# A decayed-attention kernel with a feed-forward layer: Strassen's seven products for the second token group, with its weight sums moved and taken from float16

## The chip, the cores and the metric

The kernel runs on one core of a Trainium2 chip. The metric is the device time of one execution in microseconds (us). Four runs of the kernel before gave 205.49 to 206.1 us, median 205.8 us. In this text PE is TensorE (matmul), DVE is VectorE, ACT is ScalarE, POOL is GpSimd and SP is SyncE, which issues most DMAs.

## What is computed

```python
# attention: q, k, v are (4, 8, 768, 64); blocks of 64 positions, one decay lam per head
intra = (q_b @ k_b^T) * lam^(i-j) for i >= j      # inside a block
out_b = intra @ v_b + (q_b * lam^(i+1)) @ state   # state: 64 x 64 per head
state = lam^64 * state + (k_b * lam^(63-j))^T @ v_b
# feed-forward on x = out as (3072, 512)
h = x @ w_in                # 512 -> 2048
g = gelu_tanh(h)
y = g @ w_out               # 2048 -> 512, float32 out
```

## The kernel before, in words

**Attention.** There are 24 steps `s`, each 256 positions of four heads. `prep(s)` makes float16 copies: `prep_qk` scales q on DVE (L237) and copies k on ACT (L242), `prep_v` scales v on POOL (L227). `stage_t(s)` transposes q and k on PE for `s < 9` (L258) and copies the result out of PSUM (L261 to L267; by ACT for 1, 5 and 6, by both for 2 and 3, by DVE for 0, 4, 7 and 8); later steps are transposed by a DMA from SP's queue (L246). `R(n, s)` puts on PE the scores of step n (`Sps`, L287), the key-value products of n (L322) and the outputs of step s (L336, L345), then on DVE the mask (`PT`, L296) and the state (`t`, L381, L384), and on POOL the spread state `u` (L391); `x_out` copies outputs to `xT` on ACT (L364). `U(n)` is the state step for the second block of n.

**Feed-forward.** Two steps of the same positions make one super-block of 256 tokens. The 12 super-blocks form seven groups, `[0,1] [2] [3] [4,5] [6,7] [8,9] [10,11]`; a "256-token group" is one of the second and third. `queue_group(g)` appends a group's PE work in pieces to the list `filler`, and `fill(n)` in the hand-written order at the end of the kernel (L613 to L719) takes the next n pieces. All instructions keep program order on their engine. `mm1` (L415) is one 512-column bank of `x @ w_in` (eight matmuls of 256 columns in a 256-token group) and a gelu on ACT into `gT` (L423). The second matmul has two forms:

- `mm2` (L428), for groups 0 and 1: four matmuls of 512 columns a piece, 16 for each 128 tokens, into one PSUM bank `O2ps`; ACT copies it out (L440), SP sends it.
- `product(m, p)` (L470), for groups 2 to 6: Strassen's scheme on 2 x 2 blocks (tokens by halves, the 2048 by halves, columns by halves). Seven products take the place of eight; each is eight matmuls of 256 columns (L488). Five of them need sums of blocks of g, made on DVE by `sum_g` (L456, L464) from `gT`; five need sums of blocks of w_out, `w_sum16`, made once by `sum_wout(j, m, eng)` (L120, L124) for halves j = 0 and 1. Products 4 and 3 fill PSUM bank A, 5 and 2 bank B, 1 bank C, 7 and 6 bank D. After product 2, ACT copies bank B (L495, L496) and DVE combines it with A (L499, L500); after product 1 DVE adds C (L508), after product 6 it adds D (L520), and SP sends the tile.

The order of the pieces of a 256-token group is eight `mm1`, then products 3, 4, 5, 2, 1, 7, 6. `behind(k, i0, i1)` (L572) hangs `sum_g` for rows i0 to i1 onto the k-th piece: the five sums of rows 0 to 3 follow the sixth `mm1`, the five of rows 4 to 7 follow product 3.

**Weights.** `load_wout` brings w_out in four parts of 512 rows as float32 (order 0, 2, 1, 3). `cast_wout` makes float16 parts in `w_out16`: 0 on POOL, 2 on ACT, 1 and 3 half on POOL and half on ACT (L116, L118). `sum_wout` reads the float32 parts. Before the change its five sums for j = 0 stand after `cast_wout(0)` and ahead of `fill(8)` (L672), those for j = 1 behind `U(8)`, `U(9)` and `U(10)` (L716).

**PSUM.** Six banks (`ps_M`) serve everything but the scores. A new tile takes a bank that an earlier tile gave up, and its first matmul waits until the last reader of the earlier tile is done. Which bank that is gets settled when the program is built.

Of the kernel before, what the change touches and what calls it, by code (L numbers as in the profile page):

```python
# [15 lines left out]
def kernel(  # L16
# [11 lines left out]
    pin = tc.keep_in_program_order  # L28
# [32 lines left out]
    def load_step(s):  # L61
# [3 lines left out]
        for nm, src in (("q", q), ("k", k), ("v", v)):  # L65
# [9 lines left out]
    w_out16 = w16p.tile([P, NF, DM], FP16)  # L75


    HF, HE = NF // 2, DM // 2
    w_sum16 = w16p.tile([P, 5, HF, HE], FP16)
    W_SUMS = {3: ((0, 1), ALU.subtract, (1, 1)), 4: ((1, 0), ALU.subtract, (0, 0)),  # L80
              1: ((0, 0), ALU.add, (1, 1)), 7: ((1, 0), ALU.add, (1, 1)),
              6: ((0, 0), ALU.add, (0, 1))}
    w_slot = {m: i for i, m in enumerate(W_SUMS)}
    wstage = {}
# [25 lines left out]
    def cast_wout(j, eng):  # L110
        t = wstage[("o", j)]
        for i in range(2):
            dst = w_out16[:, 4 * j + 2 * i : 4 * j + 2 * i + 2, :]
            src = t[:, 2 * i : 2 * i + 2, :]
            if eng[i] is nc.scalar:
                pin(nc.scalar.activation(out=dst, in_=src, func=AF.Copy))  # L116
            else:
                pin(nc.gpsimd.tensor_copy(out=dst, in_=src))  # L118

    def sum_wout(j, m, eng):  # L120

        (f0, e0), op, (f1, e1) = W_SUMS[m]
        a, b = wstage[("o", j + 2 * f0)], wstage[("o", j + 2 * f1)]
        pin(eng.tensor_tensor(w_sum16[:, w_slot[m], 4 * j : 4 * j + 4, :],  # L124
                              a[:, :, e0 * HE : e0 * HE + HE], b[:, :, e1 * HE : e1 * HE + HE], op))


    lam_in = const.tile([H, 1], FP32)
# [85 lines left out]
    def prep(s):  # L214
        prep_qk(s)
        prep_v(s)
# [8 lines left out]
    def prep_v(s):  # L225
        tv = a16p.tile([P, 2, HH, D], FP16, tag="v16", name=f"v16_{s}")
        pin(nc.gpsimd.tensor_tensor(wide(tv[:]), ld32[s][2][:], decay(dv, s), ALU.mult))  # L227
        a16[s] = a16[s] + (tv,)
        if s >= 6:
            load_ahead(s + 3)  # L230

    def prep_qk(s):
        q32, k32, _ = ld32[s]
        tqk = a16p.tile([P, 2, 2, HH, D], FP16, tag="qk16", name=f"qk16_{s}")
        tq, tk = tqk[:, 0], tqk[:, 1]
        q_eng = nc.gpsimd if s == 3 else nc.vector
        pin(q_eng.tensor_tensor(wide(tq), q32[:], decay(dq, s), ALU.mult))  # L237
        if s == 0:
            inverse(halves[0])
            odd(halves[1])  # L240
            inverse(halves[1])
        pin(nc.scalar.activation(out=wide(tk), in_=k32[:], func=AF.Copy))  # L242
        a16[s] = (tq, tk)
        if s >= FIRST_DMA_T:
            o = qkp.tile([P, 2, 2, 2, P], FP16, tag="qkT", name=f"qkT_{s}")
            pin(nc.sync.dma_start_transpose(out=o[:].rearrange("p a j h t -> p (a j h) t"),  # L246
                                            in_=tqk[:].rearrange("p a j h d -> p (a j h d)")))
            qkT[s] = o

    def stage_t(s):  # L250
        if s >= FIRST_DMA_T:
            return
        tq, tk = a16[s][:2]
        Tps = ps_M.tile([P, 2, 2, 2, P], FP16, tag="M", name="Tps")
        for i, t in enumerate((tq, tk)):
            for hp in range(2):
                for j in range(2):
                    pin(nc.tensor.transpose(Tps[:, i, j, hp, :], t[:, j, 2 * hp : 2 * hp + 2, :],  # L258
                                            ident[:]))
        o = qkp.tile([P, 2, 2, 2, P], FP16, tag="qkT", name=f"qkT_{s}")  # L260
        if s in (2, 3):  # L261
            pin(nc.scalar.activation(out=o[:, 0], in_=Tps[:, 0], func=AF.Copy))
            pin(nc.vector.tensor_copy(out=o[:, 1], in_=Tps[:, 1]))
        elif s in (1, 5, 6):
            pin(nc.scalar.activation(out=o[:], in_=Tps[:], func=AF.Copy))
        else:
            pin(nc.vector.tensor_copy(out=o[:], in_=Tps[:]))  # L267
        qkT[s] = o
# [131 lines left out]
    filler = []  # L400

    def queue_group(g):
        N = len(groups[g]) * SB
        NTAU = N // P
# [10 lines left out]
        def mm1(fs):  # L415
            Hps = ps_M.tile([P, per, N], FP32, tag="M", name="Hps")
            for i, f in enumerate(fs):
                for c in range(NC):
                    pin(nc.tensor.matmul(by_block(Hps[:, i, :]), w_in16[:, c, f * P : (f + 1) * P],  # L419
                                         x(c), start=(c == 0), stop=(c == NC - 1)))  # L420
            f = fs[0]
            dst = gT[:, f, :, :] if per == 2 else gT[:, f % HF, f // HF : f // HF + 1, :]
            pin(nc.scalar.activation(out=dst, in_=Hps[:], func=AF.Gelu_apprx_tanh))  # L423
# [4 lines left out]
        def mm2(tau, part):  # L428

            if not O2.get(tau):  # L430
                O2[tau] = [ps_M.tile([P, DM], FP32, tag="M", name="O2ps"), 0]
            for f in range(4 * part, 4 * part + 4):
                n = O2[tau][1]
                pin(nc.tensor.matmul(O2[tau][0][:], gT[:, f % HF, f // HF, tau * P : (tau + 1) * P],  # L434
                                     w_out16[:, f, :], start=(n == 0), stop=(n == NF - 1)))
                O2[tau][1] += 1
            if O2[tau][1] < NF:
                return
            o32 = otp.tile([P, DM], FP32, tag="o32", name="o32")
            pin(nc.scalar.activation(out=o32[:], in_=O2.pop(tau)[0][:], func=AF.Copy))  # L440
            pin(nc.sync.dma_start(out=out[row0 + tau * P : row0 + tau * P + P, :], in_=o32[:]))
# [11 lines left out]
        def block(T, F, i):  # L453
            return gT[:, i, F, T * HN : (T + 1) * HN]

        def sum_g(i0, i1):  # L456
            for m, ((T0, F0), op, (T1, F1)) in G_SUMS.items():
                if m not in gsum:
                    k = len(gsum)
                    if k % 2 == 0:  # L460
                        pairs.append(wst.tile([P, 2, HF, HN], FP16, tag="w32", name=f"gs_{g}_{m}"))
                    gsum[m] = pairs[-1][:, k % 2]
                i = slice(i0, i1)
                pin(nc.vector.tensor_tensor(gsum[m][:, i, :], block(T0, F0, i), block(T1, F1, i), op))  # L464
# [92 lines left out]
        for i in range(HF):  # L557
            for fs in ([[i, i + HF]] if per == 2 else [[i], [i + HF]]):
                filler.append(lambda fs=fs: mm1(fs))
        if g == 1:  # L560
            for tau in range(NTAU):
                for part in (0, 2, 1, 3):
                    filler.append(lambda tau=tau, part=part: mm2(tau, part))
            return
        ms = ((3, 4, 5, 2), (1, 7, 6))
        order = [(m, p) for p in range(HN // P) for m in ms[0] + ms[1]]
        if g == len(groups) - 1:
# [1 line left out]
        for m, p in order:  # L569
            filler.append(lambda m=m, p=p: product(m, p))  # L570

        def behind(k, i0, i1):  # L572

            piece = filler[at + k]

            def both():
                piece()
                sum_g(i0, i1)

            filler[at + k] = both  # L580

        at = len(filler) - len(range(HN // P)) * 7 - HF * (2 // per)
        n1 = HF * (2 // per)
        if per == 2:
            behind(5, 0, 4)
            behind(n1, 4, 8)
        else:
            behind(9, 0, 4)
            behind(13, 4, 6)
            behind(n1, 6, 8)  # L590

    def fill(n):
        for _ in range(min(n, len(filler))):
            filler.pop(0)()

    def R(n, s):
        if n is not None:
            scores(n)
        products(n, s)
        if n is not None:  # L600
            causal(n)
        if s is not None and s % 2 == 1:
            g, i = group_of[s // 2]
            if i == len(groups[g]) - 1 and g > 0:
                queue_group(g)
        if n is not None:
            update(n, 0)

    def U(n):
        update(n, 1)  # L610
# [58 lines left out]
        cast_win(j)  # L669
    DVE, ACT, POOL = nc.vector, nc.scalar, nc.gpsimd  # L670
    cast_wout(0, (POOL, POOL))
    for m in W_SUMS:  # L672
        sum_wout(0, m, DVE)
    fill(8)
    cast_wout(2, (ACT, ACT))
    cast_wout(1, (POOL, ACT))
    cast_wout(3, (POOL, ACT))
    fill(9)
    prep(4)
    stage_t(4)  # L680
    prep(5)
    fill(2)
    R(4, None)
    stage_t(5)
# [4 lines left out]
    stage_t(6)  # L689
    U(5)  # L690
    prep(7)
    fill(2)
    R(6, 5)
    U(6)
# [1 line left out]
    prep(8)  # L696
    fill(1)
    stage_t(7)
    fill(2)
    R(7, 6)  # L700
    U(7)
# [3 lines left out]
    for n in range(8, NSTEP + 1):  # L705
        m = n if n < NSTEP else None
        if m is not None:
            stage_t(n)
        if n + 2 < NSTEP:
            prep(n + 2)  # L710
        fill(2 if n <= 12 else 4)
        R(m, n - 1)
        fill(1)
        if m is not None:
            U(m)
        for p in {8: (3, 4), 9: (1, 7), 10: (6,)}.get(n, ()):  # L716
            sum_wout(1, p, DVE)
        fill(2 if n == 11 or n > 12 and n % 2 else 3)
    fill(len(filler))  # L719

# [28 lines left out]
```

## Time and profile before

| what | value |
|---|---|
| median of 4 runs | 205.8 us |
| the profiled execution | 205.92 us |
| its span in the profile | 204.1 us |
| what lies around the span | 1.82 us |
| granted PE clock | 1.0 |
| PE busy, instructions | 197.1 us (97%), 2324 |
| DVE busy | 146.1 us (72%) |
| ACT busy | 107.9 us (53%) |
| POOL busy | 68.9 us (34%) |
| `mm2` of all groups (L434) | 96 matmuls of 512 columns |
| `sum_wout` (L124) | 10 instructions, 14.8 us |

Times inside the profile are microseconds from the span's start. A row of the groups gives line, engine, operation, what it writes and reads, the shapes, the count, then busy time, mean nanoseconds of one, and the idle time ahead of them with what ended it. A row of the timeline or of the chain gives start, length, and what ran. A duration in the timeline counts from when an instruction was at the head of its engine, so one that was held up shows longer than the same instruction alone.

### The profile page before, as it was taken

How to read it: one execution, taken by the hardware profiler on the slowest of the kernel's cores; microseconds unless marked ns; L12 is line 12 of the kernel's file. 1: busy time of each engine (PE TensorE's matmuls, PEld its weight loads, DVE VectorE, ACT ScalarE, POOL GpSimd, SP SyncE). 2: the span in 40 equal slices, each digit the busy share in tenths (PEclk: the TensorE clock that was granted, in tenths of full speed). 3: DMA queues.
4: the chain of work that ended last, by engine and by line, in shares of the span. 5: the costliest groups of instructions: out<-in, count | busy, mean ns of one | idle time of the engine just before them, and what ended most of it. 6: DMA issues, size and time to landing. Idle time of an engine off the chain costs nothing.

```text
span 204.1 us, 5592 instructions
## 1 busy us (share of the span) xinstructions
PE 197.1 (97%) x2324; PEld 128.7 (63%) x2324; DVE 146.1 (72%) x274; ACT 107.9 (53%) x204; POOL 68.9 (34%) x80
## 2 busy tenths in 40 slices
PE   6988999999999999999999999999999999999993
PEld 1556544456885688644688654688654788545882
DVE  5799726867699999929997828996739773136552
ACT  2365678466873573477723377631576431666210
POOL 6486132446587850336044304214412101000000
PEclk9999999999999999999999999999999999999999
DMA  6999999999999999996449983658340003300014
GB/s 168 293 330 385 387 386 376 280 281 318 326 245 229 290 247 143 234 283 177 89 123 250 236 241 100 144 114 135 84 99 0 0 3 103 108 0 0 3 51 154
DMA packets 63945, 37.85 MB, mean 185 GB/s; under 512 B 17584, under 2 KB 59056, under 8 KB 63920
## 3 DMA queue, kind: packets, MB, share of 16 engines
q1 hardware_dynamic: 63088, 36.97, 68.8%
q10 hardware_dynamic: 832, 0.52, 0.8%
q8 instruction: 18, 0.29, 0.6%
q14 instruction: 7, 0.06, 0.1%
HBM read 27.26 MB, written 6.29 MB: 164 GB/s over the span
## 4 chain that ended last, share of the span: by engine, by line
PE 92%; DMA 2%; DVE 2%; ACT 1%; issue 1%; SPq 0%
PE Hps L419 37%; PE O2ps L434 10%; PE MB L488 8%; PE MA L488 7%; PE MD L488 7%; PE Sps L287 4%; PE MC L488 4%; PE OK L345 3%; PE Hps L534 3%; PE OK L336 3%; PE Tps L258 2%; DMA k<-in_k_dram 2%; PE idle L152 2%; PE OK L322 1%; ACT qk L242 1%; DVE PT L296 1%
## 5 line engine op out<-in xcount | busy, mean ns | idle before, releaser
L419 PE MATMUL Hps<-xT,w_in 128*128 128x512 f16 (+1 forms) x416 | 79.1, 346 | 0.0
L423 ACT ACTIVATE gT<-Hps 128x512 f16<-128x512 f32 x88 | 52.4, 596 | 22.8 <-PE Hps L419 22.0
L419 PEld LDWEIGHTS <-w_in 128*128 128x128 f16 x416 | 40.3, 98 | 33.4
L391 POOL TENSOR_TENSOR u<-t,lumask 128x256 f16<-128x256 f32 x40 | 31.3, 789 | 81.8 <-DVE t L384 53.8
L464 DVE TENSOR_TENSOR gs<-gT 128x512 f16<-128x512 f16 (+1 forms) x70 | 36.6, 586 | 10.8 <-ACT gT L423 10.6
L296 DVE TENSOR_TENSOR PT<-Sps,mask 128x1024 f16<-128x1024 f32 x24 | 29.2, 1215 | 16.9 <-PE Sps L287 16.8
L488 PEld LDWEIGHTS <-gs 128*128 128x128 f16 x360 | 34.9, 98 | 4.0
L227 POOL TENSOR_TENSOR v<-v,dv 128x512 f16<-128x512 f32 x24 | 29.5, 1230 | 4.9 <-DMA v<-in_v_dram 2.6
L364 ACT ACTIVATE xT<-OK 128x256 f16<-128x256 f32 x47 | 18.1, 454 | 20.7 <-PE OK L345 16.3
L434 PE MATMUL O2ps<-w_out,gT 128*128 128x512 f16 x96 | 21.9, 379 | 0.0
L495 ACT ACTIVATE m<-MB 128x512 f32<-128x512 f32 x9 | 5.4, 597 | 25.4 <-PE MB L488 25.4
L237 DVE TENSOR_TENSOR qk<-q,dq 128x512 f16<-128x512 f32 x23 | 18.3, 798 | 0.0
L242 ACT ACTIVATE qk<-k 128x512 f16<-128x512 f32 x24 | 15.0, 623 | 6.4 <-DMA k<-in_k_dram 6.4
L488 PE MATMUL MA<-w_sum,gT 128*128 128x256 f16 x144 | 17.5, 273 | 0.1
L488 PE MATMUL MD<-w_sum,gs 128*128 128x256 f16 x136 | 17.5, 273 | 0.0
L488 PE MATMUL MB<-w_out,gs 128*128 128x256 f16 x144 | 17.2, 273 | 0.0
L488 PEld LDWEIGHTS <-gT 128*128 128x128 f16 x144 | 14.1, 98 | 2.8 <-ACT gT L423 0.3
L434 PEld LDWEIGHTS <-gT 128*128 128x128 f16 x96 | 9.2, 98 | 9.9
L499 DVE TENSOR_TENSOR o<-MA,m 128x512 f32<-128x512 f32 x9 | 6.2, 689 | 12.7 <-ACT m L495 12.7
L384 DVE SCALAR_TENSOR_TENSOR t<-t,lamu,OK 128x64 f32<-128x64 f32 x64 | 14.6, 272 | 0.9 <-PE OK L322 0.2
L124 DVE TENSOR_TENSOR w_sum<-wo,wo 128x1024 f16<-128x1024 f32 x6 | 8.8, 1507 | 4.6 <-DMA wo<-in_moe_w_out_dram 4.6
L287 PEld LDWEIGHTS <-qkT 64*64 64x64 f16 x384 | 6.3, 108 | 8.6 <-issue 4.2
(60 smaller groups left out, 170.3 us busy)
## 6 DMA issues: line engine op xcount, KB each, us to landing
q<-in_q_dram SPq DMA_DIRECT2D x24, 256.0 KB, 5.0
k<-in_k_dram SPq DMA_DIRECT2D x24, 256.0 KB, 5.0
v<-in_v_dram SPq DMA_DIRECT2D x23, 256.0 KB, 5.2
out_dram<-o SPq DMA_DIRECT2D x22, 256.0 KB, 4.0
wo<-in_moe_w_out_dram SPq DMA_DIRECT2D x4, 1024.0 KB, 9.1
wi<-in_moe_w_in_dram SPq DMA_DIRECT2D x4, 512.0 KB, 7.5
wi<-in_moe_w_in_dram SPq DMA_DIRECT2D x2, 1024.0 KB, 12.6
v<-in_v_dram ACTq DMA_DIRECT2D x1, 256.0 KB, 4.5
```

The lines of the kernel that those rows point to most:

```text
L227: pin(nc.gpsimd.tensor_tensor(wide(tv[:]), ld32[s][2][:], decay(dv, s), ALU.mult))
L237: pin(q_eng.tensor_tensor(wide(tq), q32[:], decay(dq, s), ALU.mult))
L242: pin(nc.scalar.activation(out=wide(tk), in_=k32[:], func=AF.Copy))
L296: pin(nc.vector.tensor_tensor(t[:].rearrange("p a b c d -> p (a b) (c d)"), Ss.pop(n)[:].rearrange("p a b c d -> p (a b) (c d)"), mask[:]. ...
L364: pin(nc.scalar.activation(out=d, in_=o, func=AF.Copy))
L384: pin(nc.vector.scalar_tensor_tensor(t[:, hp, :], state[half][:, hp, :], lamu[:, 2 * half + hp : 2 * half + hp + 1], K[:, hp, :], ALU.mult ...
L391: pin(nc.gpsimd.tensor_tensor(u[:], state[half][:].unsqueeze(2).to_broadcast([P, 2, 2, D]), lumask[:, 2 * half : 2 * half + 2, :].unsqueez ...
L419: pin(nc.tensor.matmul(by_block(Hps[:, i, :]), w_in16[:, c, f * P : (f + 1) * P], x(c), start=(c == 0), stop=(c == NC - 1)))
L423: pin(nc.scalar.activation(out=dst, in_=Hps[:], func=AF.Gelu_apprx_tanh))
L434: pin(nc.tensor.matmul(O2[tau][0][:], gT[:, f % HF, f // HF, tau * P : (tau + 1) * P], w_out16[:, f, :], start=(n == 0), stop=(n == NF - 1)))
L464: pin(nc.vector.tensor_tensor(gsum[m][:, i, :], block(T0, F0, i), block(T1, F1, i), op))
L488: pin(nc.tensor.matmul(dst, lhsT, rhs, start=(i == 0), stop=(i == HF - 1), skip_group_check=True))
```

## The change

1. Group 1 gets the seven products in place of its eight `mm2` pieces (the `if g == 1` branch goes). 32 matmuls of 512 columns become 56 of 256 columns.
2. In both 256-token groups the sums of g are spread: `sum_g` takes a list `ms`. Sums 5 and 2 for rows 0 to 3 follow the sixth `mm1`; sum 5 for rows 4 to 7 follows the eighth; sum 2 for rows 4 to 7 follows product 3; sums 1 and 7 over all rows follow product 4; sum 6 over all rows follows product 5. So sums 1, 7 and 6 stand ahead of the combinations behind product 2 in DVE's queue.
3. `sum_wout` reads `w_out16` (float16) and not the float32 parts. It now waits for the casts. For j = 0 the sums stand after the casts, in the order 6, 3, 4, 1, 7, then that of j = 1 for product 6; the other four of j = 1 follow `prep(5)`, `prep(7)` and (two) `stage_t(7)`.
4. The transposes of step 8 are copied out by ACT and not by DVE.
5. The `fill` behind `U(8)` takes two pieces and not three, since group 1 has 15 pieces and not 16.

```diff
     def sum_wout(j, m, eng):
         (f0, e0), op, (f1, e1) = W_SUMS[m]
-        a, b = wstage[("o", j + 2 * f0)], wstage[("o", j + 2 * f1)]
-        pin(eng.tensor_tensor(w_sum16[:, w_slot[m], 4 * j : 4 * j + 4, :],
-                              a[:, :, e0 * HE : e0 * HE + HE], b[:, :, e1 * HE : e1 * HE + HE], op))
+        def rows(f, e):
+            f = f * HF + 4 * j
+            return w_out16[:, f : f + 4, e * HE : e * HE + HE]
+        pin(eng.tensor_tensor(w_sum16[:, w_slot[m], 4 * j : 4 * j + 4, :], rows(f0, e0), rows(f1, e1), op))
...
-        elif s in (1, 5, 6):
+        elif s in (1, 5, 6, 8):
             pin(nc.scalar.activation(out=o[:], in_=Tps[:], func=AF.Copy))
...
-        def sum_g(i0, i1):
+        def sum_g(i0, i1, ms=None):
             for m, ((T0, F0), op, (T1, F1)) in G_SUMS.items():
+                if ms and m not in ms:
+                    continue
...
-        if g == 1:
-            for tau in range(NTAU):
-                for part in (0, 2, 1, 3):
-                    filler.append(lambda tau=tau, part=part: mm2(tau, part))
-            return
...
         if per == 2:
-            behind(5, 0, 4)
-            behind(n1, 4, 8)
+            behind(5, 0, 4, (5, 2))
+            behind(7, 4, 8, (5,))
+            behind(8, 4, 8, (2,))
+            behind(9, 0, 8, (1, 7))
+            behind(10, 0, 8, (6,))
...
     cast_wout(0, (POOL, POOL))
-    for m in W_SUMS:
-        sum_wout(0, m, DVE)
     fill(8)
     cast_wout(2, (ACT, ACT))
     cast_wout(1, (POOL, ACT))
     cast_wout(3, (POOL, ACT))
+    for m in (6, 3, 4, 1, 7):
+        sum_wout(0, m, DVE)
+    sum_wout(1, 6, DVE)
     fill(9)
     prep(4)
     stage_t(4)
     prep(5)
+    sum_wout(1, 3, DVE)
...
     prep(7)
+    sum_wout(1, 4, DVE)
...
     stage_t(7)
+    sum_wout(1, 1, DVE)
+    sum_wout(1, 7, DVE)
...
-        for p in {8: (3, 4), 9: (1, 7), 10: (6,)}.get(n, ()):
-            sum_wout(1, p, DVE)
-        fill(2 if n == 11 or n > 12 and n % 2 else 3)
+        fill(2 if n in (8, 11) or n > 12 and n % 2 else 3)
```

More of the change, by code (lines that the diff above doesn't have):

```diff
@@ L570, in queue_group, with behind @@
             filler.append(lambda m=m, p=p: product(m, p))
-        def behind(k, i0, i1):
+        def behind(k, i0, i1, ms=None):
             piece = filler[at + k]
@@ L577, in both @@
                 piece()
-                sum_g(i0, i1)
+                sum_g(i0, i1, ms)
             filler[at + k] = both
```

## The prediction, on record before the result

> **What bounds the kernel now.** I read the page's busy shares and slices first, then the chain of work that ended last, then the timelines of DVE and POOL around the second group.
>
> ```profile
> PE 197.1 (97%) x2324; PEld 128.7 (63%) x2324; DVE 146.1 (72%) x274; ACT 107.9 (53%) x204; POOL 68.9 (34%) x80
> ...
> DVE  5799726867699999929997828996739773136552
> ```
>
> PE is busy for 97%. A slice is 5.1 us; DVE is full from about 56 to 87 us, where the second group's second matmul stands. In order of time the chain is PE without a gap from 21.7 us to 200.6 us, but for a wait near 76 us.
>
> ```profile
> 60.57 4.32 PE O2ps L434 x20
> 64.89 0.35 PE Sps L287 x16
> ...
> 65.92 2.59 PE O2ps L434 x12
> 68.51 2.62 PE Hps L419 x24
> ...
> 75.73 0.45 issue
> 76.18 0.62 ACT qk L242
> 76.80 0.49 ACT gT L423
> 77.29 0.05 issue
> 77.34 0.28 PE MA L488
> ...
> 100.56 1.75 PE MA L488 x16
> ```
>
> Columns are start, length, what ran, matmuls. The first and third lines are the 32 matmuls that the change replaces; the last is sixteen of the kind that replaces them. The lines near 76 us are product 3 of group 2 waiting for a gelu queued behind a k copy on ACT: five `mm1` from 72.15 and eight products should end at 77.40 and end at 77.62, so 0.22 us. So PE work taken out shortens the run one for one, if everything that PE waits for is still on time.
>
> **Step 1, the matmuls.** Out: 4.32 + 2.59 = 6.91 us for 32, 0.216 each. In: 56 at 1.75 / 16 = 0.1094, 6.13 us. Gain 0.78 us. The sixteen-matmul rows are 1.75 in every later group, so I give this no range. The Trainium skill, "TensorE: Matmul & The Clock Gate", section "Back-to-back issue gap", speaks against the change: it gives a sustained 131 ns for 512 columns and 81 ns for 128; a straight line between them gives 98 ns for 256, an estimate, and by it 56 x 98 - 32 x 131 ns would make the run 1.3 us longer. This trace has 216 and 109 ns, so the measurement decides.
>
> **Step 2, evacuation.** ACT loses two `O2ps` copies of 0.60 us and gains 0.60 + 0.38 (rows of L495, L496). Output DMAs stay two of 256 KB, issued some 2 us later on SP, ahead of step 12's DMA transpose, which waits for its q until then anyway and is needed at 83 us. Nothing.
>
> **Step 3, DVE's work and POOL.** The sums of w_out change from 1.21 us (float32 alone, 73.29 us) to the row of L464 with the same shapes.
>
> ```profile
> 73.29 1.21 DVE L124 TENSOR_TENSOR w_sum<-wo 128x1024 f16<-128x1024 f32 x1
> 74.43 0.83 DVE L464 TENSOR_TENSOR gs<-gT 128x512 f16<-128x512 f16 x1
> 75.18 1.26 DVE L464 TENSOR_TENSOR gs<-gT 128x512 f16<-128x512 f16 x1
> 76.36 0.41 DVE L464 TENSOR_TENSOR gs<-gT 128x512 f16<-128x512 f16 x1
> ```
> ```profile
> 73.51 1.47 POOL L391 TENSOR_TENSOR u<-t,lumask 128x256 f16<-128x256 f32 x1 [2.21 <-DVE t L384]
> 74.94 1.22 POOL L227 TENSOR_TENSOR v<-v,dv 128x512 f16<-128x512 f32 x1
> ```
>
> Start, length, operation, shapes. Alone, a sum of 512 takes 0.41 us (next one 0.34 on), one of 1024 takes 0.68 (next one 0.60 on), `u` 0.61, `v` 1.04. Here the `u` asked at 73.51 and ended at 74.98, 0.5 after the DVE sum ended at 74.50; the DVE sum asked at 74.43 and ended 0.28 after that `u`; the next ended 0.28 after the `v` (76.16). So a DVE operation with two SBUF inputs and a POOL operation take turns, whole instructions at a time. `PT`, `t` and the bank combinations, which read PSUM, keep 1.21, 0.27 and 0.68 beside POOL. With these turns I laid DVE's new order out by hand, on before's clock.
>
> *28 to 42 us.* The first sum needs `cast_wout(0)` (POOL, done 31.07). The next wait for `cast_wout(2)`, whose second half ends on ACT near 35.6 (33.62 plus two of 1.0). From 35.7: three sums at 0.60, a turn for POOL's cast (asked at 37.34; to 38.5), two sums, end 39.7. Before, the float32 sums ended at 39.7 too:
>
> ```profile
> 39.62 0.68 DVE L237 TENSOR_TENSOR qk<-q,dq 128x512 f16<-128x512 f32 x1
> ```
>
> So step 4's q is ready at 40.3 as before, and its transposes on PE (40.86 in the chain) lose nothing. But `v` of step 4 asks POOL at 39.87: were DVE 0.2 us later, `v` would go first, q end 0.9 later, and PE stand still some 0.65 us.
>
> *42 to 55 us.* The sums behind `prep(5)`, `prep(7)`, `stage_t(7)` fall into idle stretches of DVE (0.80, 0.99, 1.42 us). The first starts at 42.56 while `v` of step 5 asks at 42.59. If the `v` wins, `PT` of step 4 is 0.6 late, then `u`, and PE loses some 0.25. The last two wait for `v` of step 8 and push `PT` of step 7 from 54.33 to 54.5.
>
> *55 to 61 us.* ACT copies step 8's transposes in 1.02 us (row of L265) from 57.1 to 58.2; PE takes them at 58.72. Two gelus are 0.6 and 0.3 late and free of it by 59.7; the gelu of the eighth `mm1` starts at 60.61 as before and ends 61.21, and product 3 reaches its eighth matmul at 61.33: no wait. DVE now takes turns with two `u` and two `v`: q of 9 ends 57.2, q of 10 58.2, first sum 59.3, second 60.5, and `PT` of step 8 starts 60.4, not 59.18.
>
> *61 to 71 us, the tight part.* Against PE's due time without any wait: sum 5 (rows 4 to 7) ready 62.4, due 62.76; sum 2 63.1, due 63.6; sum 1 64.1, due 65.1; sum 7, behind the `v` of step 11, 65.5, due 65.97; sum 6, behind q of 11, 66.7 plus about 0.1 to be seen by PE, due 66.85. The combinations of bank A end 67.9, C 70.05, D 71.05. Six banks are alive here (A, B, step 9's two, C, D). Group 2's first `mm1` (due 67.7) and second (68.6) can have B (free at 65.2 by ACT) and A; the third (69.46) takes step 9's first, free when `t` ends at 69.44. I put 0.1 us of waiting there. So DVE, with 3.3 us of sums of g and 2.5 of combinations in place of 7.5 of float32 sums, is just in time; the margins are 0 to 0.5 us.
>
> *After 71 us* DVE has no w_out sums left (1.21 us less) and fewer sums at once; group 2's order of products and copies is otherwise the same, and the 0.22 us wait near 76 stays, since the k copy is still ahead of the gelu. The end of the kernel is untouched.
>
> **Sum.** Profiled execution 205.92 = 204.1 + 1.82. Minus 0.78, plus 0.1: 205.24. The median of the runs lies 0.12 lower, which would give 205.1; I say **205.2 us**.
>
> **The rivals.**
>
> *DVE late in the tight part.* For: the margins above, and six turns with POOL in ten us. Against: the turns are already in my times, so more than another 0.6 us is unlikely. Every tenth that DVE is late is a tenth of waiting at sum 6 or at the third `mm1`, once. 0.2 to 0.7 us: 205.4 to 205.9.
>
> *The transposes of step 4 late.* Place: 40 us. For: a cast on ACT, not a landed DMA, now starts the sums. Against: the cast's time is in the trace, and the row above shows the same 39.62 to be met. From a delay of 0.2 us on it costs 0.65: 205.9, within 0.2%.
>
> *Slower: the wrong bank.* Place: group 2's first `mm1` at 67.7 us. The profile doesn't show which bank it gets. If it is one of step 9's, its first matmul waits for `t`, which stands in DVE's queue behind the combinations of A and `PT` of step 9: 69.5, a wait of 1.8, net 1.0 us longer, 206.9; with step 9's second bank (70.45) 207.9. It decides as soon as that bank is neither A nor B. Against: both are given up earlier in program order.
>
> *The gain is not there.* Seven products could run at the weight loads' pace: 98 ns a load against 109 a matmul in the rows, so no; it has no chance of its own.
>
> **How the numbers follow.** Forecast (204.9 to 205.4) 0.55; DVE late 0.20; transposes late 0.10; wrong bank 0.10; something slower that I don't see 0.05. About 0.2% (0.41 us) can be told from no change here, so faster means below 205.39. Faster: 0.55 and two fifths of DVE late, 0.63. Same: the rest of it and the transposes, 0.22. Slower: 0.15. The range leaves out the last two cases: 204.8 (all of step 1, and the spread of runs) to 206.2.
>
> **What would show it.** In the profile after: no `O2ps` matmul after 61 us, and 56 more products of 0.109; PE's chain through step 4's transposes at 40.9 without DVE in it; `PT` of step 8 near 60.4; in the chain between 60 and 72 us at most 0.1 to 0.2 us of DVE. A DVE piece of over 0.7 us in it, a piece of `t` ahead of an `Hps` matmul, or DVE ahead of `Tps` near 41 us would show the forecast wrong, and which rival is right.

## The result and the profile after

The kernel after takes 204.77 us (median of 36 executions), the kernel before 205.44 us (median of 59, the four shown at the head among them). The ratio is 0.9967, with a 95% interval from 0.9959 to 0.9976: 0.68 us less, between 0.49 and 0.84. The forecast was 205.2 us, and its sum took 0.68 us off the profiled execution; the range began at 204.8. The move was met, the time lies 0.03 us below the range, and the way to it was not the one I gave.

The page of the kernel after, busy shares and DVE's slices (lines of the code behind L120 are three to five higher than before):

```profile
span 202.9 us, 5650 instructions
...
PE 194.5 (96%) x2348; PEld 129.4 (64%) x2348; DVE 146.0 (72%) x281; ACT 108.8 (54%) x205; POOL 66.6 (33%) x80
...
DVE  5896623889999979939997728996739773136553
```

PE has 24 more matmuls and 2.6 us less busy time; DVE does as much as before. The 2.6 us are not the gain: PE's busy time differs between profiles of one kernel as well (197.1 and 196.0 us for the kernel before, 194.5 and 195.9 for the kernel after). The chain that ended last, in order of time:

```profile
31.80 0.60 ACT gT L426
32.39 1.90 ACT w_out L116 x2
34.31 0.97 DVE w_sum L128
35.28 0.42 issue
35.70 3.32 DVE w_sum L128 x4
39.02 0.61 DVE qk L240
39.69 0.62 PE Tps L261 x8
...
57.01 6.74 DMA qkT<-qk
63.80 0.42 PE Sps L290 x16
...
67.51 2.62 PE Hps L422 x24
```

Before, this chain was PE nearly throughout. Now two other things stand in it: the early sums of w_out ahead of step 4's transposes (39.69), and at 57.0 us the DMA transposes of step 9, landing 6.7 us after their issue. PE's timeline shows the wait:

```profile
61.26 1.91 PE L493 MATMUL MB<-w_out,gs 128*128 128x256 f16 x16
63.80 0.42 PE L290 MATMUL Sps<-qkT 64*64 64x128 f16 x16 [0.63 <-DMA qkT<-qk]
```

The scores of step 9 waited 0.63 us for the transposes, and group 2's first `mm1` starts at 67.51, against 68.51 before. But that 1.00 us can't be read as the gain: at step 4's transposes this execution was 1.17 us ahead already (39.69 against 40.86), well before any product of group 1. In the two profiles PE began the first layer at 16.8 and 18.1 us. So one pair of profiles does not answer; the runs below do.

### The profile page after: what moved, and what is told of

It is laid out like the page before. It is cut to its first block, busy times and chain, and to the rows that moved or that the text cites. A ratio compares the mean times of both kernels' runs of the same rounds, so it can differ in the third digit from the quotient of the medians.

```text
span 202.9 us, 5650 instructions
## 1 busy us (share of the span) xinstructions
PE 194.5 (96%) x2348; PEld 129.4 (64%) x2348; DVE 146.0 (72%) x281; ACT 108.8 (54%) x205; POOL 66.6 (33%) x80
## 4 chain that ended last, share of the span: by engine, by line
PE 76%; DMA 10%; DVE 5%; SPq 4%; ACT 2%; issue 1%; DVEq 0%
PE Hps L422 34%; PE MD L493 8%; PE MB L493 8%; PE MA L493 7%; PE MC L493 4%; SPq L69 4%; DMA wi<-in_moe_w_in_dram 4%; PE Hps L539 3%; DMA qkT<-qk 3%; DMA k<-in_k_dram 3%; PE Sps L290 3%; DVE w_sum L128 3%; PE OK L348 3%; PE OK L339 2%; PE O2ps L437 2%
## 5 line engine op out<-in xcount | busy, mean ns | idle before, releaser
L394 POOL TENSOR_TENSOR u<-t,lumask 128x256 f16<-128x256 f32 x40 | 29.1, 733 | 82.2 <-DVE t L387 60.2
L469 DVE TENSOR_TENSOR gs<-gT 128x512 f16<-128x512 f16 (+1 forms) x74 | 44.1, 656 | 12.1 <-ACT gT L426 11.9
L493 PEld LDWEIGHTS <-gs 128*128 128x128 f16 x400 | 38.7, 98 | 4.4
L493 PE MATMUL MA<-w_sum,gT 128*128 128x256 f16 x160 | 19.5, 273 | 0.1
L493 PE MATMUL MB<-w_out,gs 128*128 128x256 f16 x160 | 19.1, 273 | 0.0
L493 PEld LDWEIGHTS <-gT 128*128 128x128 f16 x160 | 15.5, 98 | 3.2 <-ACT gT L426 0.5
L240 DVE TENSOR_TENSOR qk<-q,dq 128x512 f16<-128x512 f32 x23 | 16.3, 707 | 0.2 <-DMA q<-in_q_dram 0.2
L437 PE MATMUL O2ps<-w_out,gT 128*128 128x512 f16 x64 | 14.6, 379 | 0.0
L128 DVE TENSOR_TENSOR w_sum<-w_out 128x1024 f16<-128x1024 f16 x10 | 9.0, 940 | 6.3 <-POOL w_out L118 3.5
L290 PE MATMUL Sps<-qkT 64*64 64x128 f16 x384 | 10.0, 222 | 1.3 <-DMA qkT<-qk 0.6
```

The lines of the kernel that those rows point to most:

```text
L290: pin(nc.tensor.matmul(Sps[half64(c), hl, hp, jk, :], o[half64(hl), 1, jk, hp, half64(c)], o[half64(hl), 0, :, hp, half64(c)], start=True, ...
L394: pin(nc.gpsimd.tensor_tensor(u[:], state[half][:].unsqueeze(2).to_broadcast([P, 2, 2, D]), lumask[:, 2 * half : 2 * half + 2, :].unsqueez ...
L493: pin(nc.tensor.matmul(dst, lhsT, rhs, start=(i == 0), stop=(i == HF - 1), skip_group_check=True))
```

## The experiments

Three theories. A: PE's matmuls are the gain, cut by whatever PE next waits for. B: the lighter, earlier sums of w_out are the gain. C: DVE has room between 56 and 71 us, so order there doesn't matter. Two more came from the profile after, here called T, step 9's DMA transposes give part of the gain back, and S, the start of the kernel became shorter. (The expectations of e5 and e7 use the letters D, E and F for theories of their own.) Each ratio is to the kernel before, run beside it on the same chip.

### e1: all but the products

```diff
+        if g == 1:            # in queue_group, as before: eight mm2 pieces
...
-        fill(2 if n in (8, 11) or n > 12 and n % 2 else 3)
+        fill(2 if n == 11 or n > 12 and n % 2 else 3)
```

> Everything of the change but the products: group 1 keeps its 32 matmuls of 512 columns. Theory A (PE work is the gain: 6.91 - 6.13 = 0.78 us, minus what new waits give back): the time of before, 205.2 to 205.7 us, so 0.5 to 0.8 us above the change. Theory B (the gain comes from the lighter, earlier sums of w_out and not from the products): the time of the change, 204.6 to 205.0. Step 9's scores then stand 0.8 us later on PE, so the wait for step 9's DMA transposes (0.7 us in the profile after) should be gone or under 0.1.

Measured: 205.45 us, ratio 0.9999 (0.9981 to 1.0018). B falls: without the products the rest of the change is worth nothing that can be told. By these medians the products bring 0.68 us. As expected, e1's profile has no wait for step 9: the scores came at 63.94, after the transposes (landed at 63.5).

```profile
59.62 4.32 PE O2ps L437 x20
63.94 0.35 PE Sps L290 x16
...
67.55 2.62 PE Hps L422 x24
```

From the first matmul of group 1's second layer to group 2's first `mm1` are 7.93 us, as in both profiles of the kernel before. In the first profile after they are 7.94 (59.41 to 67.35 in its timeline, where 7.16 would have done without a wait): in that execution the waits took back all that the products gave.

### e4, f4, f1: step 9 transposed on PE, with and without the products

```diff
-    FIRST_DMA_T = 9
+    FIRST_DMA_T = 10
...
-        elif s in (1, 5, 6, 8):
+        elif s in (1, 5, 6, 8, 9):
```

f4 is e4 run again beside f1 and the change; f1 is this edit with e1's.

> Step 9 is transposed on PE and copied out by ScalarE, not by DMA; the rest is the change. PE gets eight transposes, 0.45 us more. If the 0.7 us wait at step 9's scores in the profile after stands in most executions, the time is 204.4 to 204.7, below the change; if it stands in few of them (the profiled one being special), 204.9 to 205.3. In its profile there is no DMA ahead of the scores at 63 us; whether step 10's DMA transposes then become the next wait (due at 70 us, landed near 66) is expected not to be so.

> Run e4 once more beside f1 and the change. If taking step 9 off the DMA queues is a gain in the usual execution: 204.4 to 204.6, below the change by 0.15 to 0.4 us, with fewer executions above 205.

> Run e4 (step 9 transposed on PE) without the products in group 1: its 32 matmuls of 512 columns stand again. Against e4 this is the products alone, with no DMA transposes of step 9 to wait for. If those transposes are what the products lost time to, the difference to e4 is the matmuls' 0.7 to 0.8 us: 205.15 to 205.3. If something else gives it back (VectorE, PSUM banks), it is under 0.5: below 204.95.

Measured: e4 204.47 us, ratio 0.9957 (0.9940 to 0.9974); f4 204.40 us, 0.9951 (0.9933 to 0.9969); f1 205.12 us, 0.9982 (0.9963 to 1.0002). One execution of f1 took 230.65 us; the median hardly feels it. On one chip f4 is 0.72 us below f1 (their fastest executions 0.75: 204.27 and 205.02): the products, with no wait for step 9, against 0.78 from the rows. In the two profiles PE takes 7.69 us in f4 and 8.38 in f1 for the stretch measured above, 0.69 less. In the profile of f4 the scores follow the products without a gap:

```profile
59.47 2.01 PE L493 MATMUL MA<-w_sum,gT 128*128 128x256 f16 x16
61.31 0.61 PE L261 MATMUL Tps<-ident,qk 128*128 128x128 f16 x8
61.76 1.91 PE L493 MATMUL MB<-w_out,gs 128*128 128x256 f16 x16
63.60 0.42 PE L290 MATMUL Sps<-qkT 64*64 64x128 f16 x16
```

The eight transposes cost PE 0.45 us, and still the median is 0.30 us (e4) and 0.49 us (f4, same chip as f3) below the change. An estimate from these numbers is that the edit takes away waits of 0.7 to 0.9 us. That they are owed to the products is not shown: without the products the same edit moved the median by 0.33 us (e1 to f1, on two chips, intervals overlapping), and the products are worth as much with step 9 transposed by DMA (0.68) as on PE (0.72). So T is seen in single executions, not in the medians. This version is faster than the kernel before; as for the change, all eleven executions of f4 (204.27 to 204.80) lie below the median of f3 on the same chip, while e4 is within the noise. A holds: the products are worth their matmuls where nothing late takes the place.

### f3: the change once more

> The change itself once more, on the same chip as the two beside it, for a second profile. If the wait for step 9's transposes is the usual thing: landing after 63 us and PE waiting 0.4 us or more before step 9's scores, median 204.65 to 204.9. If the first profile was an odd one: no wait there.

Measured: 204.89 us, ratio 0.9974 (0.9952 to 0.9996). In its profile the transposes landed at 63.0 us (6.4 after their issue), just in time, and there was no wait for them. What PE waited for was DVE, as the chain says:

```profile
59.74 1.21 DVE PT L299
60.95 0.28 DVE t L387 x2
61.23 0.03 issue
61.26 0.28 DVE gs L469
...
61.59 0.46 DVE t L387 x2
62.05 2.84 DVE gs L469 x3
64.89 0.60 DVE qk L240
65.49 0.61 DVE gs L469
66.10 0.05 issue
66.15 1.05 PE MD L493 x8
67.20 2.71 PE Hps L422 x24
```

This is the tight part as laid out in the prediction: the mask of step 8, the sums with `v` of step 11 between them, the q of step 11, sum 6, and product 6 on PE waiting for it. From the end of the eighth `mm1` (59.73) to group 2's first `mm1` are 7.47 us; 56 matmuls (6.13) and `R(9, 8)` (1.03) are 7.16, so PE waited 0.31: 0.09 in product 3 for the gelu of the eighth `mm1` and 0.22 for sum 6. The last line holds one wait more: the three `mm1` take 2.71 us, against 2.62 in the first profile after. The third of them started at 68.86, 0.08 late and just behind the `t` that DVE ended at 68.81:

```profile
68.35 0.46 DVE L387 SCALAR_TENSOR_TENSOR t<-t,lamu,OK 128x64 f32<-128x64 f32 x2
```

So in this execution the gain is cut by DVE, in the one above by the DMA transposes; neither profile of the change is free of waits.

### e2: the sums of g bunched as before

```diff
-            behind(5, 0, 4, (5, 2))
...
+            behind(5, 0, 4)
+            behind(n1, 4, 8)
```

> The sums of g in both 256-token groups stand as before: five behind the sixth matmul piece, five behind product 3; the rest is the change. Theory A with VectorE just in time: three more sums of 0.34 us and their turns with POOL ahead of step 8's mask put sum 5 some 0.7 to 1.0 us later against a margin of 0.3, so PE waits 0.4 to 0.8 us at product 5, and the time is 205.1 to 205.6. Theory C (VectorE has slack here, and the spreading does nothing): 204.6 to 204.9.

Measured: 206.32 us, ratio 1.0043 (1.0025 to 1.0062), slower than before. C falls, and the cost is higher than I expected. PE's timeline has product 5 stopped after four matmuls, until rows 4 to 7 of sum 5 are there:

```profile
61.39 0.60 PE L493 MATMUL MB<-w_out,gs 128*128 128x256 f16 x4
63.37 1.49 PE L493 MATMUL MB<-w_out,gs 128*128 128x256 f16 x12 [1.38 <-DVE gs L469]
```

### e3, e11: step 8's transposes copied by DVE

```diff
-        elif s in (1, 5, 6, 8):
+        elif s in (1, 5, 6):
```

e3 is this edit on the change, e11 on e5 (below).

> The transposes of step 8 are copied out by VectorE again (0.60 us more on it ahead of the tight part); the rest is the change. VectorE just in time: 0.2 to 0.6 us longer than the change where step 9's transposes don't already hold PE up, 204.9 to 205.4. VectorE with slack, or PE held up by step 9's transposes anyway: as the change, 204.6 to 204.9.

> Run e5 with the transposes of step 8 copied by VectorE. In e3 that copy cost nothing, where PE waited for step 9's transposes anyway. With that wait gone and sum 6 already 0.24 us late, 0.6 us more of VectorE should show in full: 204.9 to 205.1. If VectorE had room there: 204.4 to 204.55, as e5.

Measured: e3 204.65 us, ratio 0.9963 (0.9949 to 0.9978), as the change. e11 205.14 us, 0.998 (0.9961 to 1.0): 0.70 above e5, but 0.26 above the second run of that same kernel (f2). The copy costs nothing that can be told on the change, whose profile in e3 waits 0.30 us for step 9's DMA. That it costs something where DVE comes last is likely and not shown: 0.70 is between two chips, the intervals of e11 and f2 overlap, and e11's profile has 0.17 us of waiting for sum 6.

### e10: the sums of w_out from float32, at the new places

```diff
+        a, b = wstage[("o", j + 2 * f0)], wstage[("o", j + 2 * f1)]
```

> The sums of w_out read the float32 parts again, at the new places; the rest is the change. Each takes 1.21 us and not 0.68. Six of them from the landing of w_out on end some 1 us later than now, so step 4's q and its transposes are late; the pair ahead of step 7's mask is 1.1 us late. Theory (VectorE just in time): 0.8 to 2 us longer than the change, 205.5 to 206.8. Rival (these places have room): 204.7 to 205.0.

Measured: 206.26 us, ratio 1.0038 (1.0023 to 1.0053), 1.49 us above the change. The pair of sums ahead of step 7's mask, and after it everything on DVE, is late, and PE waits 1.3 us for sum 5 in product 5. So the float16 source is a condition of the products, though the rest of the change brings nothing without them (e1): with float32 sums the change would be slower than the kernel before.

### e5, f2, e9, e6: the DMAs around step 9's transposes

e5 issues the `v` load of step 11 behind the transposes; f2 is the same kernel again; e9 also hangs sum 6 onto product 4; e6 issues the loads of step 12 behind step 10's transposes.

```diff
+            if s == 9:                 # e5, f2, e9: behind the DMA transpose
+                load_step(11, "v")
...
+            behind(9, 0, 8, (1, 7, 6)) # e9
...
+            if s == 10:                # e6: behind the DMA transpose
+                load_step(12)
```

> The load of v for step 11 is issued behind step 9's DMA transposes and not ahead of them; the rest is the change. Theory D (the transposes of step 9 land late because SP issues them behind three loads): issue 0.6 us earlier, near 56.4 us, landing near 63.1, the 0.63 us wait at step 9's scores falls below 0.1 and the median to 204.2 to 204.55. Theory E (DMA engines full, the landing does not follow the issue): the wait stays at 0.5 us or more and the median at 204.6 to 204.9.

> Run e5 once more, the same kernel. e5 had 204.44 and its transposes of step 9 landed 4.3 us after their issue; e9, with the same order of DMAs, had 204.85 and 7.8 us. If the order of the DMAs decides, 204.3 to 204.55 and a landing under 5.5 us again; if the landing varies by itself from execution to execution, anything from 204.4 to 204.9.

> Run e5 (v of step 11 loaded behind step 9's transposes, 204.44) and sum 6 of g hung onto product 4 with sums 1 and 7, so that it stands ahead of step 11's q on VectorE. In e5's profile PE waits 0.24 us for sum 6 at product 6; ahead of the q it is ready 0.6 us earlier. Theory (VectorE's order is the last thing in the way there): the wait is gone and the median is 204.15 to 204.35. Rival (the executions that set the median have other waits, by DMA): 204.4 to 204.6.

> The loads of step 12 are issued behind step 10's DMA transposes, so nothing follows step 9's transposes into the DMA queues for some 2 us; the rest is the change. If the loads behind them share the DMA engines and stretch them (issue to landing 6.7 us against 4.4 as the median before), the landing takes 5 us or less, the wait at step 9's scores is gone and the median is 204.2 to 204.55; if the transposes are slow by themselves, the wait and 204.6 to 204.9 stay. A late k of step 12 on ScalarE may cost 0.1 to 0.3 us near 70 us.

| run | median us | ratio (95%) | issue to landing of step 9's transposes, us | PE's wait there, us |
|---|---|---|---|---|
| e5 | 204.44 | 0.9932 (0.9903 to 0.9961) | 4.3 | none |
| f2 | 204.88 | 0.9968 (0.9948 to 0.9989) | 3.2 | none |
| e9 | 204.85 | 0.9958 (0.9941 to 0.9976) | 7.8 | 0.56 |
| e6 | 204.69 | 0.9957 (0.9930 to 0.9983) | 7.1 | 0.46 |

None of these is told apart from the change (204.77 and 204.89): one kernel gave 204.44 and 204.88 in two runs. In e9's profile the wait for sum 6 is gone, but PE waited 0.52 us in product 3 for a gelu. The loads that follow the transposes are not needed to stretch them (e6: 7.1 us with nothing behind them but step 10's). The order ahead of them doesn't settle it either (e5 and e9: 4.3 and 7.8). In both profiles of the kernel before it was 4.7 and 4.9 us. In the two profiles of the change and in e1, e2, e3 and e7, whose DMAs stand in the change's order, it was 6.4 to 7.8, with the products or without (e1: 7.0); e10, in the same order but issued 2 us later, had 3.3. What makes it long stays open.

### e7, e8: step 4's q ahead of the last three early sums

```diff
-    for m in (6, 3, 4, 1, 7):
+    for m in (6, 3, 4):
...
+    prep_qk(4)
+    for m in (1, 7):
```

e7 is this on the change, e8 on e4.

> VectorE scales q of step 4 ahead of the last three early sums of w_out; the rest is the change. The 0.3 us that PE waits at step 4's transposes (near 39.7 us) goes to under 0.1. Theory F (in most executions step 9's transposes, set by DMA, are the next late thing): PE arrives 0.3 us earlier and waits 0.3 us longer, the median stays at 204.6 to 204.85. Theory PE-bound: 204.35 to 204.55.

> Both: step 9 transposed on PE (run e4, 204.47) and q of step 4 ahead of the last three sums. With step 9's DMA out of the way the 0.3 us at step 4's transposes comes off the whole: 204.1 to 204.25. If another wait takes its place (step 10's DMA transposes, VectorE in the tight part): 204.35 to 204.5.

Measured: e7 205.07 us, ratio 0.9963 (0.9937 to 0.9989); e8 204.55 us, 0.9946 (0.9921 to 0.9970). Both miss. In both profiles DVE stood still for 1.6 us until the q of step 4 had landed (it began at 37.98 and 38.08), and the sums queued behind it came later. In e7's profile step 4's transposes are on time all the same, step 9's landed at 64.06, and PE waited 1.16 us for them. In e8's the delay of the sums reached PE, through the mask and the state of step 4. So the early place is no gain where its load is late.

### b0: the kernel before, another profile

> The kernel before once more, for another profile of it. In the one before, PE's first matmul of x @ w_in started at 18.1 us, in seven of the profiles since at 16.6 to 17.3. If the start varies between executions of one program, this one starts anywhere in 16.5 to 18.2 and its end moves with it by as much; if the kernel before always starts at 18.1, part of the gain is a shorter start that the change brings.

Measured: 205.26 us, span 203.5 us, PE's first layer from 16.87 us. The start varies with the execution; S falls. And this execution has a wait that the first profile of the kernel before did not show, in its chain:

```profile
22.54 8.84 DMA wo<-in_moe_w_out_dram
...
31.89 7.47 DVE w_sum L124 x5
39.37 0.61 DVE qk L237
39.98 0.05 issue
40.02 0.62 PE Tps L258 x8
```

The early start is partly lost at step 4's transposes, where PE waits for q behind the five float32 sums. In the change the transposes begin at 39.69 and 39.84 us, so 0.2 to 0.3 us earlier; in e1, without a gain, they begin at 39.73.

## Why the prediction was right in its move and wrong in its time

**Where it failed: the base.** "Profiled execution 205.92 = 204.1 + 1.82", and "the median of the runs lies 0.12 lower". The term is the execution that everything was subtracted from. It started PE's first layer at 18.1 us, and 59 executions have their median at 205.44, 0.48 lower and not 0.12. The median of four that I went by was itself 0.36 too high: three of the four are above 205.6 us, and so are 20 of the 59. How much a start is worth shows in e5 and f2, two executions of one kernel: PE's first layer began at 16.89 and 18.14 us, and the spans are 202.6 and 203.8. My lower end, 204.8, was "all of step 1, and the spread of runs", taken from 205.8: 205.0 less some 0.2. From 205.44 all of step 1 alone gives 204.7, below that end.

**Step 1, the matmuls:** 0.78 us; the runs have 0.72 (f1 against f4), and e1 has no gain without them. Right. The 216 and 109 ns of the trace held. The sustained rate of the Trainium skill ("TensorE: Matmul & The Clock Gate", section "Back-to-back issue gap"), by which an estimate made the change slower, does not agree with these runs.

**Step 2, evacuation:** nothing; no wait for either shows in a chain after. Right.

**Step 3, 28 to 42 us:** "lose nothing". Against b0, an execution with a like start, the change is 0.2 to 0.3 us earlier here; I had seen only an execution that started too late to wait. The `v` of step 4 never went ahead of the q in the change's own profiles (q at 38.95, `v` at 39.71 in the first). DVE ahead of `Tps` near 41 us was to be the sign of late transposes. It stands in the first profile after (39.02), but in b0 too (39.37), so it tells of an early start and not of that rival.

**42 to 61 us:** the three sums fitted. `PT` of step 8 was forecast 0.17 us ahead of the end of the eighth `mm1` (60.4 against 60.57), and began 0.02 after it in f3 (59.74 against 59.72). "No wait" in product 3 was 0.09.

**61 to 71 us:** the right place, too small. The 0.1 forecast was for the third `mm1` of group 2, behind `t`, and it came: 0.08 in f3. Ahead of it PE waited another 0.31 where none was forecast, 0.22 of it for sum 6: that was to be seen 6.2 us after the eighth `mm1` ended, just in time, and was seen after 6.4. So in that execution DVE was some 0.3 us later than my sum, as in my first rival. e2 and e10 show how little room there was. The first `mm1` of group 2 did not wait, so the wrong bank did not come up.

**The end:** "untouched". From PE's last matmul to the end of the span are 3.6 us in both profiles of the kernel before and in e1's, and 3.3 to 3.4 in the other fifteen, f1's among them. So some 0.2 us between the profiles before and after lie behind the last matmul, in no term of mine; the runs don't show what they come from. f1 and f4 are alike in it, so their 0.72 is the cleaner price of the products.

**What the sum lacked:** the DMA transposes of step 9. I looked at step 12's only. Taking 0.8 us out of PE brings the scores of step 9 forward to about 63.1 us, and in the profiles with those transposes they land at 60.8 to 64.2. In the first profile after this cost 0.63 us, as much as the likeliest of my rivals, from a source that I had not listed. In the two profiles of the change PE waited 0.3 to 0.7 us more than I forecast, and yet the medians are 0.68 us apart. The profiled executions don't add up to the medians, and what does is open; so that my 0.68 came out is partly luck.

## What to carry to other kernels

When PE is full and work is taken out of it, list everything that PE meets after the cut with the time by which each was early, the DMA transposes too; past the least of these margins the gain starts to be lost. Take the base of a forecast from many runs (four were too few here) and not from the profiled execution, and look where in the kernel that execution differs. A cut on one engine may need edits on others that are worth nothing alone: here the float16 sums and the spread sums of g together gained nothing without the products (e1), and each of them missing made the change slower than the kernel it was to improve (e10, e2).

## What the runs showed of the hardware that was not expected

The same DMA transposes took from 3.2 to 7.8 us from issue to landing, in kernels with nearly or exactly the same DMAs, and their issue held SP's queue for 1.3 to 3.6 us (1.34 in f2, 3.57 in e9). The kernel's start varied by more than a microsecond (PE's first layer from 16.6 to 18.1 us) at a granted PE clock of 0.997 to 1.0, which is more than the change is worth.
